# A gated scan with routed experts: softmax sums carried with the rows, weights formed in the jobs

## The chip, the core and the metric

The kernel runs on one core of one Trainium2 chip. The core has TensorE (PE; matmuls, with a queue of weight loads, PEld), VectorE (DVE), ScalarE (ACT), GpSimd (POOL) and SyncE (SP), which issues most transfers. The metric is the device time of one run in microseconds; of the kernel before there are three runs, with a median of 746.05 us (746.03 to 747.53).

## The reference

The first part is a recurrence along time for each of 256 channels of 4 sequences of 3648 tokens; the second sends each of the 14,592 tokens to one of 16 experts, chosen as one of 4 groups and one of 4 experts in it.

```python
f = lower + (1 - lower) * sigmoid(f_logit);  h = f * h + (1 - f) * x      # per channel, in time
g_sm = exp(g_logits - max); g_sm /= g_sm.sum() + 1e-9;  g_w = g_sm[argmax]
e_sm = exp(e_logits - max); e_sm /= e_sm.sum() + 1e-9;  e_w = e_sm[argmax]   # of the chosen group
out[token] = g_w * e_w * (relu(h @ w1[g, e]) @ w2[g, e])                  # 256 -> 1024 -> 256
```

At the argmax the exponential is 1, so the weight of a token is 1 / ((sum of the group exponentials + 1e-9) x (sum of the chosen group's expert exponentials + 1e-9)).

## The kernel before, in words

**Units.** The tokens are taken in 28 units of 512 and one half unit. For each unit ScalarE forms tanh and affine parts of the gate, VectorE finishes it (gate, L250 and L271) and runs the recurrence (scans, L261, one per 128 channels), and TensorE transposes the result (L289), multiplies it with the router (L308) and transposes the logits (L321). ScalarE copies the transposed tokens into a rows tile (L291), with the token's number behind (L293).

**Routing.** It goes by groups of units: eight single units, then ten pairs, then the half unit. VectorE takes the largest logits (`mx`, `ge`), the choice as ones and zeros (`oh`, `oh16f`); TensorE ranks the tokens of each expert (L423 to L426 in the first groups), starting from the running offsets `runoff`, of one number per expert; VectorE reads off each token's place (`sc`, `posi`, L437 and L439). Five small operations (`sm`, `se`, two called `s`, and the reciprocal at L380) turn the exponentials `ex` into the weight, which is put behind the token's number in the row. A row is therefore 258 words: 256 of data, the token's number, the weight. GpSimd scatters the rows into sixteen lists in device memory by `posi` (L398). After some units `choose` picks the fullest experts (`fill`, `top`, `who`, `sel`) and `place` notes where their early rows end (`posA`, `got`).

**Jobs.** Each expert has an early job of 2 to 5 tiles of 128 rows, taken while the units are still going, and later a job for the rest; leftover rows go into a last loop. The first four early jobs work in 32 bit on rows as they were loaded (raw, tile `xr`, loaded at L970), the others in two 16-bit parts, split by VectorE and ScalarE (`xh`, `xl`, `hh`, `hl`). A job transposes its rows (L1064), does the first matmul (L1102 raw, L1133 to L1135 otherwise), the second (L1146, L1165) and scales the result by the weight in ScalarE's copy (`o`, L1177), which GpSimd scatters to the output (L1179). The weight is read from `meta`, a copy of the last two words of the rows (L1079; for a raw job the rows themselves), or, in a late job, from `info`, which is loaded.

**Order.** Up to unit 9 the program's order on TensorE, VectorE and ScalarE is written out by hand (`p1_thunks`: unit u's scans, then the routing of unit u − 1 in the steps s1, f4x, s2, f3, f4, s6, f5). SyncE and GpSimd run in written order. Later a scheduler sets the order by its own estimates, with the jobs' work put between that of the units.

## Time and profile before

| | |
|---|---|
| median of 3 runs | 746.05 us |
| profiled execution | 747.26 us |
| its span | 745.2 us, so 2.06 us lie around it |
| granted TensorE clock, mean | 0.992 |
| TensorE busy | 707.5 us |
| VectorE busy | 513.8 us |
| ScalarE busy | 444.9 us |
| GpSimd busy | 302.6 us |

An engine is busy while an instruction other than a register, branch, semaphore or DMA-issuing one is on it. The busy share is a mean over stages with different limits: the startup, in which TensorE waits for the first routings; the stretch in which units and early jobs share all engines, up to about 280 us; and the late jobs. Where a row ends with a bracket, it says how long the engine had been idle just before, and whose work ended that idle time.

### The profile page before, as it was taken

To read this page: it belongs to the slowest core of one execution; us is meant where nothing else is said; L and a number is where in the kernel's file an instruction comes from. 1 tells how busy PE (TensorE), PEld (TensorE's weight loads), DVE (VectorE), ACT (ScalarE), POOL (GpSimd) and SP (SyncE) were. 2 spreads that over 40 slices of the span, in tenths; PEclk is the share of its full clock that TensorE was granted. 3 is DMA by queue.
4 is the path that set the end of the run, shared out by engine and by line. 5 is a ranking of instruction groups with operands and counts; after the bars stand their busy time and mean duration, and the time that the engine had idled before them with its cause. 6 is when DMAs were issued, how large, how long until landed. Compare 5 with 4: busy or idle time off the path is not lost.

```text
span 745.2 us, 18005 instructions
## 1 busy us (share of the span) xinstructions
PE 707.5 (95%) x6539; PEld 582.4 (78%) x6543; DVE 513.8 (69%) x1084; ACT 444.9 (60%) x824; POOL 302.6 (41%) x330
## 2 busy tenths in 40 slices
PE   2669999999999999999999999999999999999996
PEld 1457888888888888889989676877698888767795
DVE  6989658899999966595655755467336665676630
ACT  6667767986787864554555644566346555565531
POOL 3767367668877864632212111221131311212222
PEclk9989999999999999999999999999999999999998
DMA  8988799989999872747993281753362674666100
GB/s 326 414 293 280 238 371 288 413 295 315 322 327 288 242 233 71 221 108 199 209 223 111 91 188 38 180 154 117 114 163 99 193 193 150 181 186 189 41 30 31
DMA packets 99787, 151.36 MB, mean 203 GB/s; under 512 B 59593, under 2 KB 69594, under 8 KB 96880
## 3 DMA queue, kind: packets, MB, share of 16 engines
q1 hardware_dynamic: 85408, 102.83, 47.4%
q0 software_dynamic: 11168, 30.02, 10.8%
q10 hardware_dynamic: 3120, 17.34, 6.7%
q8 instruction: 52, 0.85, 0.5%
q14 instruction: 39, 0.32, 0.1%
HBM read 112.48 MB, written 37.93 MB: 202 GB/s over the span
## 4 chain that ended last, share of the span: by engine, by line
PE 63%; DVE 13%; issue 12%; DMA 4%; ACT 3%; POOL 3%; SPq 1%; POOLq 0%; DVEq 0%; ACTq 0%
PE ps_m L1165 25%; PE ps_m L1133 6%; PE ps_m L1135 6%; PE ps_m L1134 6%; PE ps_m L1146 4%; PE ps_m L1102 4%; DVE h L261 3%; POOL out_dram L1179 3%; PE ps_p L1135 3%; PE ps_p L1133 2%; PE ps_p L289 2%; PE ps_p L1134 2%; DVE w L997 2%; DMA xs<-rows,posi 2%; DVE hl L1139 2%
## 5 line engine op out<-in xcount | busy, mean ns | idle before, releaser
L1165 PE MATMUL ps_m<-w,hh 128*128 128x256 f16 (+4 forms) x1140 | 208.9, 272 | 0.0
L1165 PE MATMUL ps_m<-w,hl 128*128 128x256 f16 (+4 forms) x676 | 180.0, 271 | 0.0
L997 DVE TENSOR_TENSOR w<-st,w 128x1024 bf16<-128x1024 f32 x112 | 135.6, 1219 | 53.5 <-ACT w L995 52.0
L398 POOL DMA_INDIRECT xs<-rows,posi x114 | 136.5, 1198 | 73.8 <-ACT rows L293 20.7
L1179 POOL DMA_INDIRECT out_dram<-o,info x61 | 64.2, 1053 | 234.3 <-ACT o L1177 198.9
L1165 PE MATMUL ps_m<-w,rows 128*128 128x256 f16 (+4 forms) x848 | 128.4, 267 | 0.0
L995 ACT CAST w<-st 128x1024 f16<-128x1024 f32 x112 | 116.0, 1045 | 15.6 <-PE ps_m L1165 11.2
L1133 PE MATMUL ps_m<-xh,w 128*128 128x256 f16 (+9 forms) x494 | 120.4, 257 | 2.4 <-DVE hl L1139 2.4
L1165 PEld LDWEIGHTS <-hh 128*128 128x128 f16 (+5 forms) x1140 | 111.3, 100 | 12.4
L1135 PE MATMUL ps_m<-xh,w 128*128 128x256 f16 (+9 forms) x494 | 120.3, 257 | 0.0
L1134 PE MATMUL ps_m<-xl,w 128*128 128x256 bf16 (+9 forms) x494 | 120.3, 257 | 0.0
L1139 DVE SCALAR_TENSOR_TENSOR hl<-ps_m,hh 128x512 bf16<-128x512 f32 (+7 forms) x107 | 71.5, 672 | 45.5 <-ACT hh L1138 45.5
L1134 PEld LDWEIGHTS <-w 128*128 128x128 f16 x800 | 78.2, 98 | 24.8 <-issue 3.0
L1133 PEld LDWEIGHTS <-w 128*128 128x128 f16 x800 | 78.2, 98 | 23.4 <-issue 1.8
L1179 POOL DMA_INDIRECT out_dram<-o,meta x47 | 54.3, 1155 | 103.6 <-ACT o L1177 82.2
L1135 PEld LDWEIGHTS <-w 128*128 128x128 bf16 x800 | 78.1, 98 | 22.7 <-issue 0.2
L1165 PEld LDWEIGHTS <-rows 128*128 128x128 f16 (+3 forms) x848 | 77.9, 100 | 10.0 <-issue 0.6
L1138 ACT ACTIVATE hh<-ps_m 128x512 f16<-128x512 f32 (+7 forms) x107 | 63.3, 592 | 34.6 <-PE ps_m L1135 33.4
L1177 ACT ACTIVATE o<-ps_m,info 128x256 f32<-128x256 f32 (+6 forms) x61 | 28.5, 468 | 82.2 <-PE ps_m L1165 65.3
L1165 PEld LDWEIGHTS <-hl 128*128 128x128 bf16 (+4 forms) x676 | 66.2, 100 | 6.9
L261 DVE TENSOR_TENSOR_SCAN h<-zt,h 128x512 f32<-128x512 f32 (+3 forms) x48 | 56.8, 1194 | 2.0 <-PE ps_p L289 1.5
L1138 ACT ACTIVATE rows<-ps_p 128x512 f16<-128x512 f32 (+7 forms) x60 | 31.0, 516 | 24.8 <-PE ps_p L1135 24.7
(209 smaller groups left out, 1211.6 us busy)
## 6 DMA issues: line engine op xcount, KB each, us to landing
st<-in_wexp_dram SPq DMA_DIRECT2D x112, 512.0 KB
zt<-in_zx_dram ACTq DMA_DIRECT2D x16, 1024.0 KB
w<-in_wexp_dram SPq DMA_DIRECT2D x16, 512.0 KB
xs<-blank SPq DMA_DIRECT2D x26, 258.0 KB
zt<-in_zx_dram SPq DMA_DIRECT2D x6, 1024.0 KB
st<-in_zx_dram SPq DMA_DIRECT2D x8, 512.0 KB
xr<-xs SPq DMA_DIRECT2D x12, 258.0 KB
xr<-xs SPq DMA_DIRECT2D x16, 129.0 KB
```

The source lines that it names most:

```text
L261: sn = nc.vector.tensor_tensor_scan(out=h[:, k, c0 - a:c1 - a], data0=ff[:, k, c0 - a:c1 - a], data1=uu[:, k, c0 - a:c1 - a], initial=init ...
L398: sc = nc.gpsimd.indirect_dma_start(out=xs_v[G["t0"] + t][:, :], out_offset=bass.IndirectOffsetOnAxis(ap=R["posi"][:, t:t + 1], axis=0), i ...
L995: nc.scalar.copy(j.wh[i], j.st[i])
L997: nc.vector.tensor_tensor(out=j.wl[i], in0=j.st[i], in1=j.wh[i], op=ALU.subtract)
L1102: nc.tensor.matmul(pm[:, n * w:(n + 1) * w], (j.wh, j.wl)[c // 4][k][:, c % 4 * P:(c % 4 + 1) * P], x[:, 0:w], start=(k == 0), stop=(k == ...
L1133: nc.tensor.matmul(po, w1_at(j.wh, k, c), xh[:, k], start=(k == 0), stop=False)
L1134: nc.tensor.matmul(po, w1_at(j.wh, k, c), xl[:, k], start=False, stop=False)
L1135: nc.tensor.matmul(po, w1_at(j.wl, k, c), xh[:, k], start=False, stop=(k == KD - 1))
L1138: eviction[0] = nc.scalar.activation(hi, pv, AF.Relu).ins
L1139: nc.vector.scalar_tensor_tensor(out=h_at(j.hl[ch], cs, slice(0, w)), in0=pv, scalar=0.0, in1=hi, op0=ALU.max, op1=ALU.subtract)
L1165: nc.tensor.matmul(pm[i * q:i * q + n, 0:dw], h_at(h[ch], [c], ts)[:, 0], w2_at(w, c)[:, i * dw:(i + 1) * dw], start=(c == 0 and s == 0), ...
L1179: nc.gpsimd.indirect_dma_start(out=out_v[out_n[0]].rearrange("n (g d) -> (n g) d", g=g), out_offset=bass.IndirectOffsetOnAxis(ap=lt[s, r, ...
```

## The change

The row grows from 258 to 262 words: behind the token's number stand the sum of the group's exponentials and, for each of the four groups, its exponentials' sum times the token's choice of the group (with the 1e-9). Routing then has two small operations per rows tile (`s6`), written straight into the rows, and no reciprocal. The weight is formed in the jobs: `shares` adds the four words, multiplies by the first and takes the reciprocal, once for each piece of up to two tiles of an early job, and once for a late job's `info`; `o` is scaled by its result `wt`. In the program text these three operations stand behind a chunk's last first-matmul eviction. Further, `f5r` (the copy of the running offsets) is taken out of `f5` and put ahead of the row copies `back(u - 1)` in the order written by hand, and the two single selections in `choose` go to GpSimd from unit 3 on.

```diff
-    RW = D + 2
+    RW = D + 6
...
+    nc.gpsimd.memset(blank.bitcast(F32)[:, D + 1:RW], 1.0)
...
             tc.keep_in_program_order(nc.scalar.activation(ex, R["ge"], AF.Exp))
 
         def s6():
-            sm = rt.tile([P, T, 5], F32, name="sm", bufs=1)
-            V.tensor_reduce(out=sm, in_=R["ex"], axis=AX, op=ALU.add)
-            se = rt.tile([P, T, 4], F32, name="se", bufs=1)
-            V.scalar_tensor_tensor(out=se, in0=sm[:, :, 1:5], scalar=1e-9, in1=R["oh"][:, :, 0, :],
-                                   op0=ALU.add, op1=ALU.mult)
-            s1_ = rt.tile([P, T], F32, name="s1")
-            V.tensor_reduce(out=s1_, in_=se, axis=AX, op=ALU.add)
-            s2_ = rt.tile([P, T], F32, name="s2")
-            V.scalar_tensor_tensor(out=s2_, in0=sm[:, :, 0], scalar=1e-9, in1=s1_, op0=ALU.add, op1=ALU.mult)
-            R["s2"] = s2_
-
-        def s8():
             at = 0
             for rows, n in G["rows"]:
-                V.reciprocal(rows[:, 0:n, D + 1], R["s2"][:, at:at + n])
+                sm = rows[:, 0:n, D + 1:RW]
+                V.tensor_reduce(out=sm, in_=R["ex"][:, at:at + n], axis=AX, op=ALU.add)
+                V.scalar_tensor_tensor(out=sm[:, :, 1:5], in0=sm[:, :, 1:5], scalar=1e-9, in1=R["oh"][:, at:at + n, 0, :],
+                                       op0=ALU.add, op1=ALU.mult)
                 at += n
 
         def s5():
...
             V.tensor_tensor(out=sc, in0=pv[:, 0:T], in1=R["oh16"], op=ALU.mult)
             posi = R["posi"] = rt.tile([P, T], I32, name="posi", bufs=4)
             placed[G["t0"]] = V.tensor_reduce(out=posi, in_=sc, axis=AX, op=ALU.add).ins
+            if not R.get("run"):
+                f5r()
+
+        def f5r():
+            pv = R["pp"][:, 0:(T + 1) * NE].rearrange("p (t e) -> p t e", e=NE)
             new = state["runoff"] = rt.tile([P, NE], F32, name="runoff")
             nc.scalar.copy(new, pv[:, T])
+            R["run"] = True
 
         if fast and T <= 4:
             s7s = [lambda t=t: s7(t, min(T, t + 4)) for t in range(0, T, 4)]
         else:
             s7s = [lambda t=t: s7(t, t + 1, t > 0) for t in range(T)]
         if fast:
-            return s1, f4x, s2, f3, f4, s6, lambda: (f5(), s8()), s7s
-        return s1, s2, s3, s4, s5, lambda: (s6(), s8()), s7s
+            f5.soon = f5r
+            return s1, f4x, s2, f3, f4, s6, f5, s7s
+        return s1, s2, s3, s4, s5, s6, s7s
 
     def p1_thunks(us, groups, parts):
         th, marks = [], {}
...
                     wave(u, 1)
                     put(lambda u=u: p1_affine(u + 1))
+                    put(f5.soon)
                     back(u - 1)
...
             picked.add(j.idx)
             unblanked.append(j)
+        B = nc.gpsimd if u >= BOOK else V
         sel = rt.tile([P, NE], F32, name="sel", bufs=6)
         cut_of = [EARLY[j.idx][0] for j in js]
         if len(set(cut_of)) > 1:
             for k, c in enumerate(cut_of):
                 one = rt.tile([P, NE], F32, name="sel", bufs=6)
-                V.tensor_scalar(out=one, in0=key, scalar1=top[:, k:k + 1], scalar2=None, op0=ALU.is_equal)
+                B.tensor_scalar(out=one, in0=key, scalar1=top[:, k:k + 1], scalar2=None, op0=ALU.is_equal)
                 chosen.setdefault(c, []).append(one)
         else:
             chosen.setdefault(cut_of[0], []).append(sel)
-        B = nc.gpsimd if u >= BOOK else V
         B.tensor_scalar(out=sel, in0=key, scalar1=top[:, len(js) - 1:len(js)], scalar2=None, op0=ALU.is_ge)
         if u >= BOOK:
             gone = rt.tile([P, NE], F32, name="gone")
...
-            j.info = mo.tile([P, MT + 1, 2], I32, name="info", bufs=6)
+            j.info = mo.tile([P, MT + 1, RW - D], I32, name="info", bufs=6)
...
-            j.meta.append(r[:, 0:m, D:D + 2])
+            j.meta.append(r[:, 0:m, D:RW])
             return
-        meta = mo.tile([P, 2, 2], I32, name="meta", bufs=16)
-        tc.keep_in_program_order(nc.vector.tensor_copy(meta[:, 0:m], r[:, 0:m, D:D + 2]))
+        meta = mo.tile([P, 2, RW - D], I32, name="meta", bufs=16)
+        tc.keep_in_program_order(nc.vector.tensor_copy(meta[:, 0:m], r[:, 0:m, D:RW]))
         if j.kind != "A":
             nc.vector.copy_predicated(out=meta[:, 0:m, 0], mask=j.mask[:, 0:m], data=nowhere[:, 0:m])
         j.meta.append(meta)
...
+
+    def shares(meta, n):
+        v = meta.bitcast(F32)
+        both = mo.tile([P, MT + 1], F32, name="both", bufs=2)
+        nc.vector.tensor_reduce(out=both[:, 0:n], in_=v[:, 0:n, 2:6], axis=AX, op=ALU.add)
+        nc.vector.scalar_tensor_tensor(out=both[:, 0:n], in0=v[:, 0:n, 1], scalar=1e-9, in1=both[:, 0:n],
+                                       op0=ALU.add, op1=ALU.mult)
+        wt = mo.tile([P, MT + 1], F32, name="wt", bufs=6)
+        nc.vector.reciprocal(wt[:, 0:n], both[:, 0:n])
+        return wt
+
+    def job_shares(j, ch):
+        if j.kind == "B":
+            n = sum(len(p) for p in j.parts)
+            if ch == 0 and n:
+                j.wt[0] = shares(j.info, n)
+            if ch == 0 and j.idx in SECOND:
+                j.wt["joint"] = shares(j.joint, 1)
+            return
+        a, w = j.chunks[ch]
+        for pi, (b, n) in enumerate(j.pieces):
+            if a <= b < a + w:
+                j.wt[pi] = shares(j.meta[pi], n // P)
 
     def raw1(j, ch, cs):
         w = j.chunks[ch][1]
...
                                        op0=ALU.max, op1=ALU.subtract)
+        if cs[-1] == KF - 1:
+            job_shares(j, ch)
 
     def raw2(j, ch, t, cs, pm):
         b, n, _ = j.parts[ch][t]
...
         o = mo.tile([P, D], F32, name="o", bufs=O_BUFS)
         if j.kind == "B":
-            lt, r = j.info, b // P
+            lt, wt, r = j.info, j.wt[0], b // P
             if g > 1:
                 r += j.tails.index((b, p, g))
         else:
             pi = max(i for i, (a, _) in enumerate(j.pieces) if a <= b)
-            lt, r = j.meta[pi], (b - j.pieces[pi][0]) // P
+            lt, wt, r = j.meta[pi], j.wt[pi], (b - j.pieces[pi][0]) // P
         s = slice(0, p if g == 1 else P)
-        nc.scalar.activation(o[s, 0:dw], pm[s, 0:dw], AF.Copy, scale=lt.bitcast(F32)[s, r, 1:2])
+        nc.scalar.activation(o[s, 0:dw], pm[s, 0:dw], AF.Copy, scale=wt[s, r:r + 1])
```

**VectorE, routing of the first unit**, before and then after. `oh16f` is the choice, `sc` and `posi` the place of each token; L261 (after: L263) is a scan.

```order
L412 TENSOR_TENSOR oh16f<-oh 128x64
L367 TENSOR_REDUCE sm<-ex 128x20
L369 SCALAR_TENSOR_TENSOR se<-sm,oh 128x16
L372 TENSOR_REDUCE s_259<-se 128x4
L374 SCALAR_TENSOR_TENSOR s_261<-sm,s_259 128x4
L437 TENSOR_TENSOR sc<-ps_p,oh16f 128x64
L439 TENSOR_REDUCE posi<-sc 128x4
L380 RECIPROCAL rows<-s_261 128x4
L250 SCALAR_TENSOR_TENSOR zt<-zt 128x512
L261 SCALAR_TENSOR_TENSOR h<-zt,h 128x512
```

```order
L405 TENSOR_TENSOR oh16f<-oh 128x64
L371 TENSOR_REDUCE rows<-ex 128x4x5
L372 SCALAR_TENSOR_TENSOR rows<-rows,oh 128x4x4
L430 TENSOR_TENSOR sc<-ps_p,oh16f 128x64
L432 TENSOR_REDUCE posi<-sc 128x4
L252 SCALAR_TENSOR_TENSOR zt<-zt 128x512
L263 SCALAR_TENSOR_TENSOR h<-zt,h 128x512
```

Between `oh16f` and the next gate (`zt`) seven rows have become four: the five that made the weight are two, and the reciprocal behind `posi` is gone.

**ScalarE, the same place.** L234 (after: L236) is the affine part of a gate, `rows` the copies of tokens and their numbers, `runoff` the running offsets.

```order
L234 ACTIVATE zt<-zt,mid,half 128x512 x2
L291 COPY rows<-ps_p 128x2x256
L293 COPY rows<-tokno 128x4
L291 COPY rows<-ps_p 128x2x256
L441 COPY runoff<-ps_p 128x16
L313 COPY rs<-ps_p 128x128
```

```order
L236 ACTIVATE zt<-zt,mid,half 128x512 x2
L439 COPY runoff<-ps_p 128x16
L293 COPY rows<-ps_p 128x2x256
L295 COPY rows<-tokno 128x4
L293 COPY rows<-ps_p 128x2x256
L315 COPY rs<-ps_p 128x128
```

The copy of the running offsets has moved from behind the three row copies to ahead of them.

**VectorE, between the routing of unit 7 and that of the first pair of units**, with the tiles' numbers. `h` are scans, `mx` to `oh16f` the routing of the pair, `xr_942`, `xr_1174` and `xr_1186` the loaded rows of raw jobs 1, 2 and 3.

```order
L271 SCALAR_TENSOR_TENSOR zt_370<-zt_370 128x1024
L261 SCALAR_TENSOR_TENSOR h_1041<-zt_370,h_929 128x512 x2
L250 SCALAR_TENSOR_TENSOR zt_372<-zt_372 128x1024
L261 SCALAR_TENSOR_TENSOR h_1142<-zt_372,h_1041 128x512 x2
L261 SCALAR_TENSOR_TENSOR h_1253<-zt_465,h_1142 128x512 x2
L335 TENSOR_REDUCE mx_1304<-Lg_1171 128x40
L337 TENSOR_TENSOR ge_1306<-Lg_1171,mx_1304 128x160
L341 SCALAR_TENSOR_TENSOR pw_1316<-ge_1306,pri_89 128x160
L343 TENSOR_REDUCE pm_1318<-pw_1316 128x40
L345 TENSOR_TENSOR oh_1320<-pw_1316,pm_1318 128x160
L412 TENSOR_TENSOR oh16f_1324<-oh_1320 128x128
```

```order
L263 SCALAR_TENSOR_TENSOR h_993<-zt_357,h_888 128x512 x2
L252 SCALAR_TENSOR_TENSOR zt_359<-zt_359 128x1024
L1099 TENSOR_REDUCE both_1342<-xr_942 128x2
L263 SCALAR_TENSOR_TENSOR h_1092<-zt_359,h_993 128x512 x2
L1100 SCALAR_TENSOR_TENSOR both_1342<-xr_942,both_1342 128x2
L1103 RECIPROCAL wt_1345<-both_1342 128x2
L1099 TENSOR_REDUCE both_1642<-xr_1174 128x2
L1100 SCALAR_TENSOR_TENSOR both_1642<-xr_1174,both_1642 128x2
L1103 RECIPROCAL wt_1645<-both_1642 128x2
L263 SCALAR_TENSOR_TENSOR h_1203<-zt_445,h_1092 128x512 x2
L1099 TENSOR_REDUCE both_1838<-xr_1186 128x2
L1100 SCALAR_TENSOR_TENSOR both_1838<-xr_1186,both_1838 128x2
```

The sums of three raw jobs now stand between the scans; those of job 2 stand ahead of the last two scans, those of job 3 behind them. One row further (the reciprocal) `mx` of the pair follows.

**VectorE, the routing of a pair of units in the full stretch.** `meta` are the last words of a job's rows, `both` behind `meta` and `wt` those of the new sums.

```order
L367 TENSOR_REDUCE sm<-ex 128x40
L391 TENSOR_TENSOR sc<-scn,both 128x128
L369 SCALAR_TENSOR_TENSOR se<-sm,oh 128x32
L660 SCALAR_TENSOR_TENSOR fill<-both,least 128x16
L392 TENSOR_TENSOR sc<-sc,oh_3408 128x128
L372 TENSOR_REDUCE s_3581<-se 128x8
L662 MAX top<-fill 128x8
L394 TENSOR_REDUCE posi<-sc 128x8
L374 SCALAR_TENSOR_TENSOR s_3583<-sm,s_3581 128x8
L664 MAX_INDEX who<-top,fill 128x8
L706 SCALAR_TENSOR_TENSOR posA<-both,taken 128x16
L380 RECIPROCAL rows<-s_3583 128x4 x2
```

```order
L385 TENSOR_TENSOR sc<-sc,oh_3367 128x128
L372 SCALAR_TENSOR_TENSOR rows<-rows,oh 128x4x4
L661 SCALAR_TENSOR_TENSOR fill<-both,least 128x16
L387 TENSOR_REDUCE posi<-sc 128x8
L663 MAX top<-fill 128x8
L707 SCALAR_TENSOR_TENSOR posA<-both,taken 128x16
L263 SCALAR_TENSOR_TENSOR h<-zt,h 128x512
L665 MAX_INDEX who<-top,fill 128x8
L712 SCALAR_TENSOR_TENSOR got<-posA,eoff 128x16
L1099 TENSOR_REDUCE both<-meta 128x2 x2
L1100 SCALAR_TENSOR_TENSOR both<-meta,both 128x2 x2
L1103 RECIPROCAL wt<-both 128x2 x2
```

The weight's `sm`, `se`, two `s` and two reciprocals are replaced by two pairs (of which the last row stands here as L372), and six operations for two pieces of a job stand behind them.

## Rows read from the trace of the kernel before

**Rows 1.** The page, busy us of each engine (share of the span) and instructions.
```profile
PE 707.5 (95%) x6539; PEld 582.4 (78%) x6543; DVE 513.8 (69%) x1084; ACT 444.9 (60%) x824; POOL 302.6 (41%) x330
```

**Rows 2.** Stretches: length, then busy us per engine (instructions), PEclk, DMA share, GB/s.
```profile
40.00:60.00 20.00, 13.77 (x114) 10.92 (x113) 18.55 (x52) 14.41 (x32) 13.26 (x18) 0.83 0.86 302
...
80.00:100.00 20.00, 20.00 (x152) 16.64 (x151) 12.15 (x30) 13.90 (x31) 7.33 (x12) 1.00 0.80 262
...
600.00:700.00 100.00, 100.00 (x881) 77.28 (x880) 64.87 (x118) 57.79 (x100) 19.95 (x19) 1.00 0.58 167
```

**Rows 3.** The same view for the stretch in which VectorE is full.
```profile
132.71:255.47 122.76, 119.78 (x1248) 104.27 (x1248) 121.47 (x243) 101.57 (x192) 92.54 (x86) 1.00 0.93 315
```

**Rows 4.** Waits of TensorE, 24 to 62 us: total us, times, longest.
```profile
PE ps_p L424 <- DVE oh16f L412: 10.6, 5, 3.2
```

**Rows 5.** TensorE, timeline: start, us, line, operation, [idle before <-releaser].
```profile
28.60 0.32 PE L426 MATMUL ps_p<-oh16f,ones 128*128 128x64 bf16 x4
```

**Rows 6.** VectorE, timeline of the startup.
```profile
29.20 0.22 DVE L437 TENSOR_TENSOR sc<-ps_p,oh16f 128x64 f32<-128x64 f32 x1
...
29.59 0.17 DVE L380 RECIPROCAL rows<-s 128x4 f32<-128x4 f32 x1
29.67 1.25 DVE L261 TENSOR_TENSOR_SCAN h<-zt,h 128x512 f32<-128x512 f32 x1
...
31.52 0.18 DVE L660 SCALAR_TENSOR_TENSOR fill<-runoff,least 128x16 f32<-128x16 f32 x1 [0.59 <-ACT runoff L441]
31.73 0.18 DVE L662 MAX8 top<-fill 128x8 f32<-128x16 f32 x1
...
39.04 0.18 DVE L706 SCALAR_TENSOR_TENSOR posA<-runoff,taken 128x16 int32<-128x16 f32 x1 [0.53 <-ACT runoff L441]
...
39.93 0.35 DVE L674 TENSOR_SCALAR sel<-fill,top 128x16 f32<-128x16 f32 x2
```

**Rows 7.** VectorE, timeline, the routing of unit 5.
```profile
51.99 0.17 DVE L372 TENSOR_REDUCE s<-se 128x4 f32<-128x16 f32 x1
...
52.75 1.19 DVE L271 SCALAR_TENSOR_TENSOR st<-st 128x1024 f32<-128x1024 f32 x1
...
54.60 0.17 DVE L706 SCALAR_TENSOR_TENSOR posA<-runoff,taken 128x16 int32<-128x16 f32 x1 [0.65 <-ACT runoff L441]
```

**Rows 8.** TensorE, timeline, its last wait in the startup.
```profile
60.38 0.19 PE L424 MATMUL ps_p<-oh16f,upto 128*128 128x64 bf16 x1 [0.75 <-DVE oh16f L412]
```

**Rows 9.** SyncE, timeline: the loads of raw jobs' rows and the stores behind them.
```profile
66.75 0.93 SPq L970 DMA_DIRECT2D xr<-xs  x2
71.67 0.36 SPq L697 DMA_DIRECT2D xs<-blank  x1
...
80.13 1.21 SPq L970 DMA_DIRECT2D xr<-xs  x2
...
82.50 0.96 SPq L970 DMA_DIRECT2D xr<-xs  x2
...
85.89 0.36 SPq L697 DMA_DIRECT2D xs<-blank  x1
```

**Rows 10.** VectorE, timeline, 70 to 92 us.
```profile
70.48 2.46 DVE L261 TENSOR_TENSOR_SCAN h<-zt,h 128x512 f32<-128x512 f32 x2
...
83.11 0.32 DVE L335 TENSOR_REDUCE mx<-Lg 128x40 f32<-128x160 f32 x1 [2.50 <-ACT Lg L322]
...
84.89 0.29 DVE L412 TENSOR_TENSOR oh16f<-oh 128x128 bf16<-128x128 f32 x1
```

**Rows 11.** TensorE, timeline, the ranking of the first double group.
```profile
87.42 0.23 PE L424 MATMUL ps_p<-oh16f,upto 128*128 128x128 bf16 x1
```

**Rows 12.** VectorE, timeline, in the full stretch.
```profile
218.55 0.16 DVE L660 SCALAR_TENSOR_TENSOR fill<-both,least 128x16 f32<-128x16 f32 x1
218.63 0.28 DVE L392 TENSOR_TENSOR sc<-sc,oh 128x128 f32<-128x128 f32 x1
```

**Rows 13.** Waits of TensorE, 130 to 260 us.
```profile
PE ps_m L1133 <- DVE hl L1139: 2.1, 2, 1.1
```

More of the change, by code (lines that the diff above doesn't have):

```diff
@@ L140, in gated_scan_moe @@
     nc.gpsimd.memset(nowhere, N)
-    dmat = iota_f32("dmat", [P], [[1, P]], mult=-1)
+    dmat = p1.tile([P, P], F32, name="rs")
+    nc.gpsimd.iota(dmat, pattern=[[1, P]], base=0, channel_multiplier=-1, allow_small_or_imprecise_dtypes=True)
     tri = const.tile([P, P], BF16, name="tri")
@@ L335, in s1 @@
             V.tensor_reduce(out=mx, in_=lg, axis=AX, op=ALU.max)
-            ge = R["ge"] = rt.tile([P, T, 5, 4], F32, name="ge")
+            ge = R["ge"] = rt.tile([P, T, 5, 4], F32, name="ge", bufs=1)
             V.tensor_tensor(out=ge, in0=lg, in1=mx[:, :, :, None].broadcast_to([P, T, 5, 4]), op=ALU.subtract)
@@ L343, in s2 @@
             V.tensor_reduce(out=pm, in_=pw, axis=AX, op=ALU.max)
-            oh = R["oh"] = rt.tile([P, T, 5, 4], F32, name="oh")
+            oh = R["oh"] = rt.tile([P, T, 5, 4], F32, name="oh", bufs=1)
             V.tensor_tensor(out=oh, in0=pw, in1=pm[:, :, :, None].broadcast_to([P, T, 5, 4]), op=ALU.is_equal)
@@ L933, in job_rows @@
                 if j.idx in PAIRS:
-                    joint[j.idx] = mo.tile([P, 2], I32, name="joint", bufs=2)
+                    joint[j.idx] = mo.tile([P, 1, RW - D], I32, name="joint", bufs=2)
                 j.joint = joint[SECOND.get(j.idx, j.idx)]
-                sync.dma_start(out=j.joint[at:at + n], in_=xs[bass.ds(pos + b, n), D:D + 2])
+                sync.dma_start(out=j.joint[at:at + n, 0], in_=xs[bass.ds(pos + b, n), D:RW])
             full = [p for ps_ in j.parts for p in ps_ if p[2] == 1]
@@ L1025, in job_xt @@
                                             scalar2=float(at - b), op0=ALU.subtract, op1=ALU.is_ge)
-                    nc.vector.copy_predicated(out=j.joint[s, 0:1], mask=gone[s], data=nowhere[s, 0:1])
+                    nc.vector.copy_predicated(out=j.joint[s, 0, 0:1], mask=gone[s], data=nowhere[s, 0:1])
                 if nf:
@@ L1075, in job_xt @@
         if j.raw:
-            j.meta.append(r[:, 0:m, D:D + 2])
+            j.meta.append(r[:, 0:m, D:RW])
             return
-        meta = mo.tile([P, 2, 2], I32, name="meta", bufs=16)
-        tc.keep_in_program_order(nc.vector.tensor_copy(meta[:, 0:m], r[:, 0:m, D:D + 2]))
+        meta = mo.tile([P, 2, RW - D], I32, name="meta", bufs=16)
+        tc.keep_in_program_order(nc.vector.tensor_copy(meta[:, 0:m], r[:, 0:m, D:RW]))
         if j.kind != "A":
@@ L1140, in m1_step @@
                                        op0=ALU.max, op1=ALU.subtract)
+        if cs[-1] == KF - 1:
+            job_shares(j, ch)
     def raw2(j, ch, t, cs, pm):
@@ L1203, in m2_joint @@
         o = mo.tile([P, D], F32, name="o", bufs=O_BUFS)
-        nc.scalar.activation(o, pm[:, 0:D], AF.Copy, scale=b.joint.bitcast(F32)[:, 1:2])
-        nc.gpsimd.indirect_dma_start(out=out_v[out_n[0]], out_offset=bass.IndirectOffsetOnAxis(ap=b.joint[:, 0:1], axis=0),
+        nc.scalar.activation(o, pm[:, 0:D], AF.Copy, scale=b.wt["joint"][:, 0:1])
+        nc.gpsimd.indirect_dma_start(out=out_v[out_n[0]], out_offset=bass.IndirectOffsetOnAxis(ap=b.joint[:, 0, 0:1], axis=0),
                                      in_=o, in_offset=None, bounds_check=N - 1, oob_is_err=False)
```

7 lines of the change are left out of this document (4 added, 3 removed).

## The prediction

> **What bounds the kernel now.** I read the page's busy times first, then a table by stage, then the waits of the engine that is late in each stage, and last the instructions around those waits. TensorE is busy 95% of the span and VectorE 69% [rows 1]. By stage they differ. In the startup, 40 to 60 us, VectorE works 18.55 of 20 us and TensorE only 13.77; from 80 to 100 us and again from 600 to 700 us TensorE has no gap, while VectorE has much room [rows 2]. Between lies a third stage, 132.71 to 255.47 us: VectorE is busy 121.47 of 122.76 us and TensorE 119.78 [rows 3]. So VectorE's time is TensorE's time in the startup, VectorE has room from some 62 to 130 us and behind 256 us, and in the third stage each further microsecond on it should come out at TensorE once. What TensorE waits for up to 62 us is one thing: L424, the matmul that ranks the tokens, for oh16f, five times, 10.6 us in all [rows 4]. What stands ahead of oh16f on VectorE is therefore the price of the startup.
>
> **Startup: weights taken out of the routing.** Each of the first routings has five small operations (sm, se, s, s, reciprocal), the changed one two. sc cannot start before TensorE's L426 ends, at 28.60 + 0.32 = 28.92 [rows 5]; I set it at 28.96, where it was at 29.20 [rows 6]: 0.24. The reciprocal holds the next scan by 29.67 − 29.59 = 0.08 [rows 6]. So 0.32 a routing, five routings ahead of the last oh16f that TensorE waits for, and 0.03 more in the first of them: −1.63. Half would be the least (sc later than I set it), 2.0 the most.
>
> **Startup: the running offsets copied earlier.** VectorE stands still 0.59 us before fill and 0.53 before posA for ScalarE's runoff copy, which is queued behind two row copies of the unit before [rows 6]. With the copy ahead of them these go; with the 0.08 to 0.09 by which an unheld operation starts before its forerunner ends, −0.68 and −0.61. Late next there is VectorE itself.
>
> **Startup: the two single selections.** L674's pair lasts 0.35 [rows 6], and what follows starts 0.09 before its end: −0.26. On GpSimd they stand behind the choice and before the next scatter; I cost them at nothing, since TensorE waits for nothing of GpSimd's there [rows 4]. Without that cover it is at most twice VectorE's 0.35.
>
> **Startup: the routing of unit 5.** The gate that started at 52.75 can start where the third small operation did, at 51.99; then posA, which waited 0.65 us for the copy until 54.60, comes at about 53.33, since sc and posi now stand behind the gate and fill that gap [rows 7]. −1.27. Against it, job 0's three new operations (its rows are read as they were loaded) stand ahead of the next routing: +0.51, three operations at 0.17. Sum of the startup on VectorE: −1.63 − 0.68 − 0.61 − 0.26 − 1.27 + 0.51 = −3.94. TensorE gets the same: its 0.75 us of waiting at 60.38 [rows 8] covers what the last steps give beyond the first 3.2. I take −3.9; bounds −3.0 and −4.6.
>
> **A new wait at 80 to 90 us.** The three sums of a raw job read the tile that SyncE's load fills. In the changed order VectorE meets those of job 2 ahead of a pair of scans, and those of job 3 ahead of the mx of the first double group. VectorE is in order, so behind job 2's operation stand both scans, job 3's operations, mx and the chain to oh16f, for which TensorE's L424 waits. When does the data come? Job 2's two loads are issued from 80.13 to 81.34, job 3's from 82.50 to 83.46. The blank store that waits for job 3's goes at 85.89, 2.4 us behind the issue; the one for job 1 went at 71.67, 4.0 behind 67.68 [rows 9]. So job 2's rows are there between 83.75 and 85.35; I take 83.75, by the example that lies nearest in time. Then 0.5 for the three sums, 2.46 for two scans, 0.5 again, and 83.11 to 85.18 from mx to oh16f, 2.07 [rows 10]: 89.3. TensorE began L424 at 87.42 without waiting [rows 11], so 1.9 are lost, and TensorE has no gap in this stage in which to make them good [rows 2]. If loads landed as soon as issued it would be 86.9 and cost nothing; with 85.35 it is 3.5. I take +1.8. This presumes that the loads move forward with the startup, as TensorE and ScalarE do.
>
> **The full stretch, 132.71 to 255.47.** Five double groups lose two operations each (six become four), ten in all, at 0.11, between the two paces that follow: −1.1. Eleven job pieces add three each, of which 31 operations fall in the stretch. An operation that needs nothing of its forerunner starts 0.08 behind it though both last 0.16 to 0.28 (fill at 218.55, sc at 218.63) [rows 12]; a dependent one 0.21 (fill at 31.52, top at 31.73) [rows 6]. The scheduler put pairs of pieces side by side, so I take 0.09 on average, +2.75, and 0.1 for the wider copies of the row tail: +1.75. Bounds 0.5 and 3.5. Passed on in full, since TensorE waits for hl, the VectorE half of an activation, for 2.1 us [rows 13].
>
> The row shows 0.08 between independent starts [rows 12]. The Trainium skill, "VectorE: DVE Perf Modes", section "The DRAIN you can't avoid", says that the next operation does not start until the pipe is empty, and its rules ask for few operations. By that each of the 21 operations added net would cost its full 0.17, 3.6 in place of 1.75, and the sum would be 1.8 longer; the trace disagrees for the independent ones.
>
> **Behind 256 us** TensorE is at 100% and VectorE at 65 of 100 us [rows 2]; the sixteen late jobs' sums lie in those gaps. +0.2 for the short stage in which the late jobs are ordered; bounds 0 and 0.5. Wider rows change no count of descriptors; nothing.
>
> Sum: −3.9 + 1.8 + 1.75 + 0.2 = −0.15. The profiled execution took 747.26 us and the median of three is 746.05, so I carry the difference over to the median: 745.9. As the first 0.1 to 0.3 of VectorE's added time can fall into its 1.29 us of idle time in the stretch [rows 3], I state 745.7.
>
> **Rivals.** (1) The gain is kept: the rows of jobs 2 and 3 land early enough and the added operations fill the spaces between waiting ones. −3.9 + 0 + 0.5 = −3.4: 742.7. For it: the pace of 0.08, and 1.29 us of idle VectorE. Against it: the load to blank store times of 2.4 and 4.0 us. (2) Slower: the load of job 2 holds VectorE for longer than I think, because it hangs on GpSimd's scatters and moves less than TensorE does, or lands after 4.0 us. From a stall of 3.45 on the sum is over +1.5; with 4.0 it is −3.9 + 4.0 + 1.75 + 0.2 = +2.05: 748.1. For it: one of the two landing times. Against it: the other one, and that the wait can shrink with the startup. (3) Every added operation costs its duration in the full stretch: +1.85 on the sum, 747.7. For it: the dependent pace of 0.2; against it [rows 12]. (4) The change does in the startup little of what it should, because TensorE meets job 0's loads or the scatters instead of oh16f: −1 instead of −3.9, 748.8. Against it: the waits name oh16f alone [rows 4].
>
> **Chances.** My forecast, within about 1.5 us of before: 0.39. Rival 1: 0.33. Rival 2: 0.16, rival 3: 0.07, rival 4: 0.05. A difference of under 0.2%, 1.5 us, is about what a measurement of this kernel cannot tell from none. So faster 0.33, within 0.2% 0.39, slower 0.28. The likeliest case's own range is 744.6 to 747.5; with most of the rivals 742.6 to 748.6.
>
> **What would show it.** In the changed profile: the routing's small operations are two per tile and VectorE's waits for runoff are gone; L424's waits in the startup sum to some 7 us; at 75 to 90 us VectorE waits for a DMA into xr at L1099 for some 5 to 9 us and TensorE for oh16f for 1 to 3; in the full stretch TensorE's waits for hl grow by 1 to 3 us; from 300 us on nothing changes. I am wrong if that wait for xr does not come up at TensorE, if hl's waits do not grow, or if the first expert's matmuls start less than 3 us earlier.

## The result, and the profile after

The changed kernel takes 756.78 us (755.88 to 757.32, 4 runs), the one before beside it 746.35 (746.03 to 747.53, 4 runs): 1.0138 times as long, with a 95% interval of 1.0122 to 1.0154. The forecast was 745.7, with a range to 748.6; the change is slower than any case in it, its four rivals included (748.8 at most). The profiled run took 757.22 us over a span of 755.2, against 747.26 and 745.2.

The page's busy times, for comparison with [rows 1]:

```profile
PE 711.0 (94%) x6539; PEld 584.3 (77%) x6543; DVE 521.4 (69%) x1185; ACT 445.2 (59%) x824; POOL 306.6 (41%) x333
```

TensorE is busy 3.5 us longer with the same number of matmuls, and the rest of the 10 us is idle time. To see where, I took the start of each matmul after less the start of the same matmul before. This *offset* is used in all that follows (plus is later than before; places are those of the kernel before, and matmuls that stand in another order are left out):

| place in the kernel before | offset, us | step, us |
|---|---|---|
| 68 to 86 us | −0.75 | −0.75, the startup |
| 87.4 us, then 90 to 125 us | +3.6, then +5.92 | +6.7, a wait (4.3) and a slow clock (2.3) |
| 127 us, then 131 us | +7.17, then +8.42 | +2.5, two waits of ScalarE |
| 256 us | +9.70 | +1.3, the full stretch |
| end | +9.78 | +0.1 |

Each kernel has one trace, and in the startup an offset can be out by 1 us. Experiment 8 shows it: up to 39.5 us its five engines run the same instructions in the same order as in the kernel before, and its offset at 36 to 40 us is −1.01.

**The startup.** Waits of TensorE, 24 to 62 us, of after, and VectorE's timeline (start, us, line, operation):

```profile
PE ps_p L417 <- DVE oh16f L405: 8.0, 4, 2.9
```

```profile
29.94 0.23 DVE L430 TENSOR_TENSOR sc<-ps_p,oh16f 128x64 f32<-128x64 f32 x1 [0.39 <-ACT runoff L439]
...
30.34 1.27 DVE L263 TENSOR_TENSOR_SCAN h<-zt,h 128x512 f32<-128x512 f32 x1
31.53 0.15 DVE L661 SCALAR_TENSOR_TENSOR fill<-runoff,least 128x16 f32<-128x16 f32 x1
...
36.88 0.22 DVE L430 TENSOR_TENSOR sc<-ps_p,oh16f 128x64 f32<-128x64 f32 x1 [0.42 <-ACT runoff L439]
...
38.47 0.15 DVE L707 SCALAR_TENSOR_TENSOR posA<-runoff,taken 128x16 int32<-128x16 f32 x1
```

TensorE's wait for oh16f fell from 10.6 to 8.0 us [rows 4], and `fill` and `posA` no longer wait, as forecast. But `sc` now stands still for ScalarE's copy of the running offsets: both read the same tile in PSUM (the memory that TensorE writes), and the copy comes first in the program. ScalarE's timeline shows why it isn't there at once: TensorE's counts end at 29.60, and ScalarE is at the affine part of a gate until 29.85.

```profile
28.35 1.50 ACT L236 ACTIVATE st<-st,mid,half 128x512 f32<-128x512 f32 x2
29.76 0.15 ACT L439 COPY runoff<-ps_p 128x16 f32<-128x16 f32 x1
```

From `oh16f` (28.94) to the scan it is 1.40 us; before it was 1.37. Nothing is left there of what the routing saved. The first such wait of `sc` is earlier, 0.70 us at 16.44; up to 45 us there are five, 2.4 us in all.

**The new wait at 76 to 91 us.** VectorE's timeline:

```profile
75.91 0.14 DVE L1100 SCALAR_TENSOR_TENSOR both<-xr,both 128x2 f32<-128x2 f32 x1
76.08 0.17 DVE L1103 RECIPROCAL wt<-both 128x2 f32<-128x2 f32 x1
85.19 0.16 DVE L1099 TENSOR_REDUCE both<-xr 128x2 f32<-128x8 f32 x1 [8.94 <-DMA xr<-xs]
...
88.47 0.16 DVE L1099 TENSOR_REDUCE both<-xr 128x2 f32<-128x8 f32 x1 [0.36 <-DMA xr<-xs]
```

SyncE's timeline, which answers to [rows 9]:

```profile
67.12 0.94 SPq L972 DMA_DIRECT2D xr<-xs  x2
...
82.48 2.91 SPq L972 DMA_DIRECT2D xr<-xs  x4
```

TensorE's timeline, which answers to [rows 11]:

```profile
91.05 0.27 PE L417 MATMUL ps_p<-oh16f,upto 128*128 128x128 bf16 x1 [4.25 <-DVE oh16f L405]
...
91.90 1.06 PE L1127 MATMUL ps_m<-xh,w 128*128 128x256 f32 x2
```

Job 2's load is issued at 82.48, 2.35 us later than before [rows 9], though TensorE is 0.75 ahead. It lands 2.7 us behind its issue; I had taken 3.6 (80.13 to 83.75). VectorE has stood 8.94 us in front of job 2's sum, with both scans, job 3's sums and the first pair's routing behind it, and TensorE loses 4.25 us at L417. What follows is in the windows of after (length, then busy us of PE, PEld, DVE, ACT, POOL, PEclk, DMA share, GB/s):

```profile
88.00:90.00 2.00, 0.00 (x0) 0.00 (x0) 1.46 (x8) 0.37 (x2) 0.00 (x0) 0.76 0.22 74
90.00:92.00 2.00, 0.95 (x11) 0.95 (x11) 1.93 (x4) 0.44 (x1) 0.00 (x0) 0.50 0.93 136
92.00:94.00 2.00, 2.00 (x6) 1.58 (x6) 1.90 (x3) 1.28 (x2) 0.00 (x0) 0.50 0.74 186
94.00:96.00 2.00, 2.00 (x8) 1.52 (x6) 1.56 (x7) 0.45 (x1) 0.16 (x1) 0.54 1.00 397
96.00:98.00 2.00, 2.00 (x24) 1.57 (x23) 0.41 (x1) 2.00 (x6) 1.70 (x2) 1.00 1.05 438
```

The granted clock fell while TensorE had nothing to do (0.76 from 88 to 90 us) and was at its lower level (0.50, 1.2 GHz) from 90 to nearly 96 us; a pair of 256-column matmuls took 1.06 us there, against 0.59 in experiment 7, where the clock stayed at 1.00. From 91.05 to 95.90 us each matmul adds to the offset, 2.3 us in all. The wait and the clock together are the +6.7.

**ScalarE at 131 to 137 us.** ScalarE's timeline:

```profile
130.98 1.04 ACT L997 CAST w<-st 128x1024 f16<-128x1024 f32 x1 [2.08 <-DMA st<-in_wexp_dram]
...
137.44 0.33 ACTq L212 DMA_DIRECT2D zt<-in_zx_dram  x1
137.82 0.60 ACT L1130 ACTIVATE hl<-ps_m 128x512 f32<-128x512 f32 x1 [4.17 <-DMA xs<-blank]
```

ScalarE first waits 2.08 us for a weight tile, and then 4.17 us to issue its own load of a later unit's gate inputs, which has to wait for a blank store that SyncE issued at 128.87. `hl` (an activation half of a job) stands behind it. TensorE shows it in two places:

```profile
133.71 0.33 PE L323 MATMUL ps_p<-ident,rs 128*128 128x128 f32 x1 [0.73 <-ACT rows L293]
...
138.48 1.13 PE L1175 MATMUL ps_m<-w,hl 128*128 128x256 f32 x4 [0.98 <-ACT hl L1130]
```

**The full stretch**, the same instructions as in [rows 3], and TensorE's waits from 140 to 340 us:

```profile
141.12:265.17 124.05, 119.97 (x1248) 104.49 (x1248) 122.90 (x263) 102.01 (x192) 88.73 (x85) 1.00 0.92 313
```

```profile
PE ps_m L1160 <- DVE hl L1166: 3.8, 6, 1.1
```

It is 1.29 us longer, and the waits for `hl` are 3.8 us; in the kernel before they are 2.1 in [rows 13] and 2.4 from 130 to 330 us, the same stretch of work.

### The profile page after: what moved, and what is told of

Its sections match the earlier page's. It is cut to its first block, busy times and chain, and to the rows that moved or that the text cites. A ratio compares the mean times of both kernels' runs of the same rounds, so it can differ in the third digit from the quotient of the medians.

```text
span 755.2 us, 18085 instructions
## 1 busy us (share of the span) xinstructions
PE 711.0 (94%) x6539; PEld 584.3 (77%) x6543; DVE 521.4 (69%) x1185; ACT 445.2 (59%) x824; POOL 306.6 (41%) x333
## 4 chain that ended last, share of the span: by engine, by line
PE 58%; issue 12%; DVE 11%; DMA 9%; POOL 4%; ACT 3%; SPq 1%; POOLq 0%; DVEq 0%; ACTq 0%
PE ps_m L1194 25%; PE ps_m L1160 6%; PE ps_m L1162 6%; PE ps_m L1161 6%; DMA zt<-in_zx_dram 3%; POOL out_dram L1208 3%; DMA st<-in_wexp_dram 3%; PE ps_p L1162 3%; DVE h L263 3%; PE ps_p L1160 3%; PE ps_p L1161 3%; DVE w L999 2%; PE ps_p L291 2%; DVE hl L1166 2%; PE ps_m L1127 1%
## 5 line engine op out<-in xcount | busy, mean ns | idle before, releaser
L391 POOL DMA_INDIRECT xs<-rows,posi x114 | 134.8, 1183 | 92.7 <-issue 19.3
L1208 POOL DMA_INDIRECT out_dram<-o,info x61 | 65.8, 1078 | 233.6 <-ACT o L1206 203.6
L1206 ACT ACTIVATE o<-ps_m,wt 128x256 f32<-128x256 f32 (+6 forms) x116 | 54.8, 474 | 129.5 <-PE ps_m L1194 100.5
L1208 POOL DMA_INDIRECT out_dram<-o,meta x47 | 51.9, 1105 | 103.3 <-ACT o L1206 80.4
L263 DVE TENSOR_TENSOR_SCAN h<-zt,h 128x512 f32<-128x512 f32 (+3 forms) x48 | 56.7, 1194 | 0.6
```

What stands on the lines that cost most here:

```text
L263: sn = nc.vector.tensor_tensor_scan(out=h[:, k, c0 - a:c1 - a], data0=ff[:, k, c0 - a:c1 - a], data1=uu[:, k, c0 - a:c1 - a], initial=init ...
L391: sc = nc.gpsimd.indirect_dma_start(out=xs_v[G["t0"] + t][:, :], out_offset=bass.IndirectOffsetOnAxis(ap=R["posi"][:, t:t + 1], axis=0), i ...
L1206: nc.scalar.activation(o[s, 0:dw], pm[s, 0:dw], AF.Copy, scale=wt[s, r:r + 1])
L1208: nc.gpsimd.indirect_dma_start(out=out_v[out_n[0]].rearrange("n (g d) -> (n g) d", g=g), out_offset=bass.IndirectOffsetOnAxis(ap=lt[s, r, ...
```

## The experiments

Each kernel was timed beside the one before. The ratio is to that kernel, with its 95% interval.

**1. The raw jobs' sums kept where the program has them** (behind a chunk's last eviction), all else as in the changed kernel.

```diff
-        nc.vector.tensor_reduce(out=both[:, 0:n], in_=v[:, 0:n, 2:6], axis=AX, op=ALU.add)
+        first = nc.vector.tensor_reduce(out=both[:, 0:n], in_=v[:, 0:n, 2:6], axis=AX, op=ALU.add)
+        if late:                     # late = j.raw
+            tc.keep_in_program_order(first)
```

> The changed kernel, with the three sums of a raw job kept on VectorE behind all that stands ahead of them in the program text, so that those of jobs 2 and 3 no longer stand ahead of the scans and of the routing of the first pair of units. Theory A (VectorE's 8.9 us wait for job 2's rows at L1099 starves TensorE of oh16f, halves its clock, and by the lateness causes ScalarE's 4.2 us wait at 133 us): the offset of TensorE against the kernel before stays at about -0.8 us past 90 us, and the loss at 126 to 130 us goes as well; +1.3 in the full stretch remains. About 746.7 us (745.5 to 748). Rival B (the scatters, late on GpSimd because of the selections there, are the cause; the sums only stand where the wait shows): job 2's rows still come at about 85.2 us and TensorE, which transposes them at about 85, stalls there for most of the same time: 751 to 756 us.

751.16 us, 1.0055 (1.0037 to 1.0073). VectorE has no wait for `xr`, the clock is 1.00 from 88 to 96 us, and the offset is +0.07 from 95 to 125 us instead of +5.92. So the wait of the sums and the clock behind it are 5.6 of the 10.4 us. ScalarE's wait stays (4.33 us), so it doesn't come from the lateness, and the time is 4.5 us above the 746.7 expected. The startup's −1.12 at 75 us isn't kept: TensorE itself waits for raw rows at 85 us (0.6 us), since their load is as late as in the changed kernel (83.32).

**2. The selections back on VectorE.**

```diff
-                B.tensor_scalar(out=one, in0=key, scalar1=top[:, k:k + 1], ...)
+                V.tensor_scalar(out=one, in0=key, scalar1=top[:, k:k + 1], ...)
```

> The changed kernel, with the single selections (L676) back on VectorE. Theory A: VectorE's startup is 0.26 us longer; GpSimd's stretch from 44 to 50 us shortens by about 1 us or more, job 2's load starts 1 to 2.4 us earlier, and so the wait for it and TensorE's stall shrink by as much: 753 to 756 us. Rival B: with the scatters in time the whole loss at 90 us goes, about 747 to 749 us.

757.59 us, 1.0126 (1.0096 to 1.0156). Job 2's load is issued at 83.13, no earlier, and the wait is 9.03 us: GpSimd's selections are not what makes the load late.

**3. The running offsets copied behind the rows again.**

```diff
-                    put(f5.soon)
                     back(u - 1)
```

> The changed kernel, with the copy of the running offsets back behind the row copies. Theory C (the early copy gives nothing, because sc, which reads the same PSUM tile, now waits for it: 0.4 to 0.7 us in each of the first routings, as much as the removed waits for it and the removed operations are worth): the startup becomes at most 0.5 us longer or up to 1 us shorter, 756 to 757.5 us. Rival D (the early copy gives the 2.5 us counted for it and something else lost them): 759 us.

753.09 us, 1.0068 (1.0045 to 1.0091). The offset is −1.23 at 75 us, +5.99 behind the wait (9.42 us, clock 0.50 from 90 to 96 us), and still so at 150 us: nothing is lost at 126 to 131 us. So without the early copy the wait of the sums is all there, and ScalarE's is not. Neither expected time (756 to 757.5, 759) came: both left ScalarE's wait out.

**4. The weights alone**, sums in program order, copy and selections as before.

> Only the sums carried with the rows and the weights formed in the jobs, with the raw jobs' sums late; the copy of the running offsets and the selections as before. Theories A and C: the startup gains what the removed small operations give, 1.3 to 1.9 us, the full stretch costs 1.3: 745 to 746.5 us, at or just below the kernel before. Rival B agrees here; a rival E (the longer rows themselves cost time in the scatters or loads) gives over 748 us.

748.3 us, 1.0022 (1.001 to 1.0035). The offset is −2.66 at 75 us, −2.16 up to 150 us and −1.14 from 256 us on in the profiled run: the startup gain is near the forecast for these steps (−1.63 − 1.27 = −2.9; job 0's sums, +0.51, come later here), and the full stretch costs 1.0. The timed runs do not show the 1.1 us that is left: the profiled run, 745.93, is the fastest of ten, and their median is 1.25 us above that of the kernel before. That is where the rival of the longer rows was put (over 748); experiment 10, with the same rows, is at 747.41. Whether the rows cost time stays open.

**5. The early copy alone**, in the kernel before.

```diff
+            if not R.get("run"):
+                f5r()
+        def f5r():
...
             new = state["runoff"] = rt.tile([P, NE], F32, name="runoff")
             nc.scalar.copy(new, pv[:, T])
+            R["run"] = True
...
+                    put(f5.soon)
                     back(u - 1)
```

> The kernel before, with the early copy of the running offsets alone. Theory C (sc now waits for that copy, since it stands behind it and reads the same PSUM tile): VectorE waits at sc in the first routings for 2 to 3 us in all and the waits of fill and posA go, startup -0.5 to +1 us; if the early copy is also what brings ScalarE's wait for the blank store at 130 us, 2.9 more: 746.5 to 750. Rival D (the copy gives what was counted for it): about 744.5.

751.21 us, 1.0058 (1.0041 to 1.0075). The offset is −1.05 at 75 us; then TensorE waits 1.6 us for job 1's rows (+0.9 up to 125 us), and ScalarE's wait at its load is there again, 5.0 us, with +3.92 from 131 us on. This small part of the change, alone, makes the kernel 4.4 us slower.

**6. The early copy ahead of the rows but behind sc and posi**, in the kernel before.

```diff
+                    put(s6)
+                    put(f5)
                     back(u - 1)
                     put(bound)
-                    put(s6)
-                    put(f5)
+                    put(f5.weights)
```

> The kernel before, with the copy of the running offsets ahead of the row copies but behind sc and posi in the program, so that sc need not wait for it. Theory C: the waits of fill and posA for the copy (0.59, 0.53 and 0.65 us) go and none takes their place: TensorE 1 to 1.7 us earlier from 60 us on, about 745 us. Rival F (ScalarE, which now waits for sc ahead of the row copies, delays the scatters and so job 2's rows): 746 to 748 us.

749.12 us, 1.0027 (1.0016 to 1.0039). The startup is 1.91 us ahead at 75 us (−1.05 with the copy ahead of `sc`), no operation of VectorE waits for the copy, and ScalarE's load doesn't wait. But the gain isn't kept. TensorE's timeline and windows of this kernel:

```profile
76.37 0.63 PE L1067 MATMUL ps_p<-ident,xr 128*128 128x128 f32 x3 [2.75 <-DMA xr<-xs]
```

```profile
78.00:80.00 2.00, 2.00 (x8) 1.56 (x7) 0.00 (x0) 0.42 (x1) 0.00 (x0) 0.50 0.86 203
80.00:82.00 2.00, 2.00 (x9) 1.72 (x8) 1.56 (x2) 0.64 (x2) 0.97 (x1) 0.71 0.93 365
```

Job 1's rows have not moved forward with TensorE: the load is issued at 68.26 (66.75 before), when GpSimd has scattered the rows. Behind the wait the clock falls here too, and the offset goes from −1.91 at 75 us to +2.79 at 79 us; so this run says little of what the copy alone is worth.

**7. Unit 6's places ahead of unit 8's gate** on VectorE, in the changed kernel.

```diff
-        pinned(u, nc.vector.scalar_tensor_tensor(out=U["x"][:, :, 0:w], ...))
+        with tc.issue_after(placed[24]) if u == 8 else ExitStack():
+            pinned(u, nc.vector.scalar_tensor_tensor(out=U["x"][:, :, 0:w], ...))
```

> The changed kernel, with unit 8's gate put behind the places of unit 6 on VectorE, as it stood before the change. Theory G (the load of job 2's rows came 2.35 us later by the clock, and 3.1 later against TensorE, because unit 6's places now stand behind a gate and a scan, and GpSimd then scatters units 6 and 7 without a gap): the load starts at 80 to 81 us, VectorE's wait for it shrinks by 1.5 to 2.5 us, and so does TensorE's stall of 4.25: 752 to 755 us. Rival H (the scatters are late already from 44 to 50 us on, where GpSimd's small operations take 0.65 to 2.4 us): the load stays at 82 us and the time at 756 to 757.

752.5 us, 1.0067 (1.0045 to 1.0089). Its loads and VectorE's wait:

```profile
79.81 3.13 SPq L973 DMA_DIRECT2D xr<-xs  x4
```

```profile
84.26 0.16 DVE L1100 TENSOR_REDUCE both<-xr 128x2 f32<-128x8 f32 x1 [5.59 <-DMA xr<-xs]
```

The load comes 2.67 us earlier, the wait is 3.35 shorter, the clock stays at 1.00, and the offset is +2.26 from 95 to 125 us. So job 2's load is late because VectorE forms unit 6's `posi` behind a gate and a scan, and the scatters, and then the load, stand behind it. VectorE in the changed kernel, and then in the kernel before:

```profile
61.13 1.23 DVE L273 SCALAR_TENSOR_TENSOR zt<-zt 128x1024 f32<-128x1024 f32 x1 [0.95 <-DMA w<-in_wexp_dram]
...
63.66 0.19 DVE L432 TENSOR_REDUCE posi<-sc 128x4 int32<-128x64 f32 x1
```

```profile
60.96 0.22 DVE L439 TENSOR_REDUCE posi<-sc 128x4 int32<-128x64 f32 x1
```

With the load in time the ranking matmul waits 1.52 us. The time is not better for all of it: at 126 us TensorE loses 3.06 us (+2.26 to +5.32), though ScalarE's load does not wait here, behind ScalarE's wait for a weight tile:

```profile
128.71 1.04 ACT L998 CAST w<-st 128x1024 f16<-128x1024 f32 x1 [3.46 <-DMA st<-in_wexp_dram]
```

**8. The selections alone on GpSimd**, in the kernel before.

> The kernel before, with the single selections alone on GpSimd. Theory H: VectorE's startup is 0.26 us shorter, but GpSimd's chain at 44 us is 0.5 to 3 us longer and the scatters behind it later: 745.5 to 747.5 us. Rival (it is free on GpSimd): 745.8.

747.14 us, 1.0015 (1.0001 to 1.003). The offset is −1.01 us at 40 us, where no selection has been moved yet (the first stands at 39.93 before), −0.58 at 75 us and −0.83 at the end. So the trace doesn't tell what the selections give (0.26 forecast), and the whole time is not shorter.

**9. Matmuls that keep TensorE busy in the wait**, in the changed kernel.

```diff
+            if G["t0"] * P == 8 * UNIT:
+                keep_warm(bank("m2"), 40)
```

> The changed kernel, with 40 matmuls of 128 columns, whose result nobody reads, on TensorE just ahead of the ranking of the first pair of units, that is in the 4.25 us in which it waits for oh16f. Theory A: the stall stays, but the clock does not fall to half behind it (0.50 from 90 to 96 us in the changed kernel), and the 2.3 us by which TensorE falls behind from 91 to 95 us are saved: about 754.5 us. Rival (what follows the stall waits for other things anyway): 756 to 757 us, or longer by the added matmuls.

752.65 us, 1.0068 (1.0051 to 1.0085): shorter than the 754.5 expected, and not for the reason expected. Its timeline and windows:

```profile
87.01 2.40 PE L300 MATMUL ps_m<-upto,tri 128*128 128x128 bf16 x40
...
91.82 0.22 PE L419 MATMUL ps_p<-oh16f,upto 128*128 128x128 bf16 x1 [1.97 <-DVE oh16f L405]
```

```profile
90.00:92.00 2.00, 0.18 (x4) 0.18 (x4) 1.83 (x7) 0.81 (x2) 0.00 (x0) 1.00 0.60 155
92.00:94.00 2.00, 2.00 (x15) 1.66 (x13) 1.90 (x2) 1.18 (x2) 0.00 (x0) 0.62 0.88 201
94.00:96.00 2.00, 2.00 (x8) 1.52 (x7) 2.00 (x7) 0.00 (x0) 0.00 (x0) 0.53 0.99 385
```

The matmuls took 2.40 us, 1.97 stayed idle, and the clock fell all the same, later. The offset is +6.06 at 95 us (+5.92 in the changed kernel). The 4.1 us come from elsewhere. ScalarE's wait at its load isn't there in this kernel, and by 131 us the offset is +6.15 in place of +8.42: 2.3 of them. The rest comes later, most of it at 141 to 145 us, where the matmuls stand in another order; what gives it is not shown.

**10. Late sums and the copy behind**: 1 and 3 together, which leaves the weights and the selections.

> The changed kernel with both undone that cost most in the runs so far: the raw jobs' sums late, and the copy of the running offsets behind the row copies; what stays of the change is the longer rows, the weights formed in the jobs and the selections on GpSimd. If the losses add (5.6 us for the wait of the sums, 3.7 for the early copy), about 747.5 us, the same as the kernel before within 1.5 us. Rival (they overlap, or the rows of jobs 1 and 2 come late for TensorE itself): 749 us or more.

747.41 us, 1.0007 (0.9996 to 1.0017): no difference from before. The two losses (5.6 us in 1, 3.7 in 3) add, and together they are all of it. The startup's −2.77 is given back at once (−0.32 at 80 us):

```profile
74.94 0.62 PE L1065 MATMUL ps_p<-ident,xr 128*128 128x128 f32 x3 [2.18 <-DMA xr<-xs]
```

**Why ScalarE's load waits.** The trace's records of the transfers name the semaphore (a counter that a transfer raises when it has landed) on which each reports. SyncE's and ScalarE's transfers have eight, dealt in turn in the order of the program, and a transfer waits until the one before it on its semaphore has landed. For the zt load in question:

```
kernel               load issued  semaphore  transfer before on it, issued   ScalarE's wait
before                 124.61       103       weight load, 117.53              none
changed kernel         137.44       104       second blank store, 128.87       4.17
late_sums              131.49       104       second blank store, 123.50       4.33
sel_on_vectore         138.00       104       second blank store, 129.41       4.6
copy_alone             132.95       104       second blank store, 123.69       5.0
copy_behind            130.60       103       weight load, 123.86              none
copy_between           129.57       103       weight load, 121.32              none
places_first           130.03       103       weight load, 122.39              none
sel_alone              124.02       103       weight load, 116.95              none
warm_stall             127.92       103       zt load, 116.34                  none
```

(weights_late_only and late_and_behind are as the last but one.) The four kernels that wait are the four in which the load shares a semaphore with the blank store. In the changed kernel the store's last count on it comes at 137.37 us, and the load goes at 137.44. The order there has one zt load and six weight loads between the two, so that eight steps on the semaphore is the same.

**11 and 12. One weight load split in two halves**, behind the blank stores (job 5) or ahead of them (job 4), in the kernel of 1.

```diff
-        sync.dma_start(out=st, in_=wexp[bass.ds(e * P, P), i * 1024:(i + 1) * 1024])
+        halves = (slice(0, 512), slice(512, 1024)) if (j.kind, j.idx, i) == ("A", 5, 1) else (slice(0, 1024),)
+        for s in halves:
+            sync.dma_start(out=st[:, s], in_=wexp[bass.ds(e * P, P), i * 1024 + s.start:i * 1024 + s.stop])
```

> The changed kernel with the raw jobs' sums held to the program's order (751.2 us, with ScalarE 4.3 us behind its own zt load at 127 to 132) and one weight load, the second of the job whose weights follow the pair of blank stores, split into two halves. Theory R (a transfer is dealt one of eight semaphores in turn and waits until the transfer eight places back in the program has landed; the zt load stood exactly eight behind the second blank store, which lands some 8 us after its issue): the split puts the zt load nine places behind it, on the semaphore of an earlier zt load that landed long before; ScalarE's wait for the blank store is gone, TensorE's offset stays at about 0 from 95 to 150 us, time about 748.3 (747.5 to 749). Rival Q (the load waits for its buffer, or the queue is full): an extra transfer changes nothing or adds to it; the wait of about 4 us stays, 751 to 752.

> The same kernel and the same split, of a weight load of the job before, which stands ahead of the two blank stores. The number of transfers is the same as in the other; the zt load and the second blank store both move on by one semaphore and still share one. Theory R: ScalarE waits for the blank store as before, 4.0 to 4.6 us, time 751.2 (750.5 to 752). Rival S (splitting a weight load is what helps, by its smaller transfers): the wait goes here too, about 748.3.

Behind: the load has semaphore 105, last used by a zt load issued at 119.05, and the wait is gone. Ahead: load and blank store are both on 105, and ScalarE's timeline has

```profile
131.64 0.60 ACT L1134 ACTIVATE hl<-ps_m 128x512 f32<-128x512 f32 x1 [4.32 <-DMA xs<-blank]
```

Theory R is shown for the wait. Its times (748.3 and 751.2) are not: 764.74 (1.0100, 1.0066 to 1.0134) and 764.47 us (1.0088, 1.0059 to 1.0117), with the kernel before itself at 755.39 in this comparison. At the place of the wait TensorE gains 1.4 us (the offset against late_sums goes from +2.94 to +1.54), not 2.9; by 145 us it is at +3.32. Between the two kernels themselves no gain is left: from 125 to 145 us TensorE loses 3.5 us in the one without the wait and 2.1 in the other. The other part of the loss at 126 to 131 us, some 1.2 us, is ScalarE's wait for the weight tile (2.28 us here, 2.08 in the changed kernel), which stays.

## Why the prediction was wrong

1. **The startup, −3.9, came as −0.75, outside its bounds.** The step that failed is "the running offsets copied earlier", with "Late next there is VectorE itself". The copy moved ahead of `sc`, which reads the same tile, and the weights' saving brings VectorE to `sc` sooner, to stand there: 2.4 us in the startup, in place of the 1.29 that the step was to give. The changed order of ScalarE was in front of me (`runoff` ahead of `rows`); I asked who waits for the copy, and not who is made to wait behind it. The Trainium skill, "PSUM — Partial Sum Buffer", section "PSUM bank collisions raise a hardware error", says that two engines may not access one bank and partition group at the same time, two reads included, and that the compiler's back end orders such instructions. The trace agrees: six times up to 68 us `sc` is released by the copy, after 0.39 to 0.95 us, 3.4 us in all; in experiment 6, where the copy stands behind `sc`, no such wait is left.

   How much of the missing 3.2 us is this step's is not settled. Of two pairs of kernels that differ in the early copy alone, one puts its cost at 75 us at 1.7 us (−2.77 in 10, −1.12 in 1), the other at 0.5 (−1.23 in 3, −0.75 in the changed kernel); and 3 and 10 run the same operations on all engines up to 56 us, yet are at −1.27 and −2.16 at 50 us. The weights alone gave −2.66 (4; −2.9 forecast), the copy in the right place −1.91 (6; −1.29 forecast), each good to about 1 us; the selections' share was not measured.

2. **The new wait, +1.8, came as +6.7.** The chain was right: VectorE's wait for `xr`, what is queued behind it, TensorE at the ranking matmul. The sentence that failed is "This presumes that the loads move forward with the startup". TensorE came 0.75 us forward and the load went back by 2.35, since `posi` of unit 6 had gone behind a gate (7): 3.1 us apart. With the 1.9 worked out, and 0.9 less for the landing, that is 4.1; TensorE's wait is 4.25. The other 2.4 of the 6.7 are, but for 0.1, matmuls that took longer until 96 us at the lower clock, which had no term at all. Where its condition held, the term came near: in 7, with the load issued at 79.81, the ranking matmul waits 1.52 us. Rival 2, with a chance of 0.16, named this mechanism and nearly this wait (4.0 us); its 748.1 fell short by the startup (3.2), the clock (2.4) and point 3 (2.5).

3. **ScalarE's waits at 126 to 131 us, +2.5, were in no term.** Half is a load that was dealt the blank store's semaphore, half a weight tile that landed late, for a cause that was not looked for; in 7 such a tile alone cost 3.06. I counted what a moved step issues on its own engine; I did not ask what the new order does to transfers that are not in the change.

4. **The full stretch, +1.75, came as +1.3**, and the waits for `hl` rose by 1.4 us (1 to 3 forecast). The pace between independent starts, and not the full duration, was the right price. The section of the Trainium skill that the prediction quotes against it, "The DRAIN you can't avoid" of "VectorE: DVE Perf Modes", goes on: "A next op that is not held starts earlier". The trace agrees with that, by the 0.08 us of [rows 12]; the prediction had left it out. **Behind 256 us**, +0.1 for +0.2.

The rest of the forecast's signs held: `fill`'s and `posA`'s waits went, L417's waits in the startup are 8.0 us (some 7 forecast), VectorE waits 9 us for `xr` (5 to 9), and from 300 us on nothing changes. One of the conditions that I named for being wrong also came: the first expert's matmuls start 1.07 us earlier, not 3.

Nor does a faster startup shorten the kernel by itself. In 5, 6 and 10 TensorE next waits for job 1's rows, 1.6 to 2.8 us: they hang on GpSimd's scatters and on a load, and these did not move with it. In 4 it waits there for only 0.2 us (the offset loses 0.5), the full stretch then takes 1.0, and the timed runs show no gain. No version tried is faster than the kernel before.

## What to carry to other kernels

When an instruction is moved forward, list the readers and writers of everything it touches: an instruction that reads the same tile may be made to wait behind it. A wait added to an engine that runs in order costs what is queued behind it, so the time at which its data comes has to be traced back to the instruction that makes it, in the new order, before its price is set. And before counting a gain ahead of a transfer's data, find what releases the transfer.
